# Two stacked expert layers behind a causal convolution: the sums of a block's end, the splits and the taps in another order

## The chip, the cores and the metric

The kernel runs on one core of one Trainium2 chip. The metric is the device time of one execution in microseconds (us), the median of several runs. TensorE (PE) multiplies, ScalarE (ACT) and VectorE (DVE) work on what it leaves in PSUM, GpSimd (POOL) helps at the start, and SyncE (SP) issues most transfers. Each engine takes its instructions in the order in which they stand in its queue.

## What is computed

The input `x` is 2 x 4096 x 192 in fp32. The cut reference:

```python
# layer "conv": softmax of 7 taps per head (8 heads of 24 channels), causal along the sequence
w = exp(weight - max(weight)); w = w / (sum(w) + 1e-09)
y[b, s, c] = sum_k w[head(c), k] * x_pad[b, s + k, c]
# first layer, 8192 tokens, 192 -> 2048 -> 192, weights in fp64
h = y @ w_in;  y1 = (h * sigmoid(h)) @ w_out
# second layer, the same shapes
h = y1 @ w_in2; out = where(h > 0, h, exp(min(h, 0)) - 1) @ w_out2
```

## The kernel before

Channels lie on partitions and tokens along the free dimension. 8192 tokens make 16 blocks of 512 (`b`); the 2048 hidden channels make 8 groups of 256 (`q`). A **unit** is (layer, block, q), 256 units in all: layer 0 is the SiLU layer, layer 1 the ELU layer. Each value is carried as a high and a low part. In layer 0 blocks 0 to 2 are computed with wide parts; from block 3 (`NEW`) on, in both layers, parts in fp16 with a scale per block are used for what goes into the second product, and in layer 0 also for `x` and both weights (the **narrow** weights, made by `rescale_in` and `rescale_out` from the wide ones during units 19 to 31).

**A unit.** `in_products` (line 595) makes `h`, two PSUM banks, of which there are two pairs; so the `h` of a unit can begin only when the `h` of two units ago has been read for the last time. `act_steps` then issues, in layer 0, Silu (ACT, line 643), the high part `g_hi` (ACT, 635) and the low part `lo` (DVE, 638), which reads `h` last. In layer 1 it issues Relu and Exp (ACT, 646 and 647), the joining `g` (DVE, 648), which reads `h` last, and then the high and low parts of the unit before, which were held back.

**Sums.** `high_products` (707) and `low_ab` (729) add a unit's part to four PSUM banks: `c0`, `c1` (64 of the 192 output channels and their low parts) and `ab0`, `ab1` (the other 128), the two of a name being the sums of two halves of the rows. Products trail `h` by three units (`LATE`). A **block's end** is the step whose trailing unit has q = 7: there `end_products` issues the block's low `c` products (719), the last high ones and the last `low_ab`, and the four banks have to be emptied before the next block opens them. `end_steps` returns `end_c` and `end_ab`: each copies one half with ACT (line 837, into `both`, `mid_ab` or `o`) and adds the other with DVE (line 828). `emit_end_c` then folds the two row halves of `both` into `other` (ACT 861, DVE 863). Layer 0 stores `mid_ab` and `other` to a buffer in DRAM, layer 1 stores `o` and `other` as the output.

**Work beside it.** `fill` is a table written by hand: `at(step, f, part)` files a piece of work under a unit's step and a part, and `run_fill(step, parts)` issues it. In an ordinary step all of a step's parts come ahead of the unit's activations; at a block's end part 0 comes ahead of them, part 1 between `end_c` and `end_ab`, and part 2 last. It holds the convolution's **taps** of later blocks (`conv_steps`, 14 per block, on DVE, lines 544 and 546), `found_it` (the reductions of `x`, 463), `set_scale` (line 486 and six more small DVE operations, giving `x_up`), `split_conv` (ACT 376, DVE 377: the two parts of a block's `x`, then exchanges of row halves by SP, 337), `split_mid` (the same for layer 1, from the stored block: two ACT copies, two DVE subtractions, a reduction, exchanges), and the decoding of layer 1's weights (`made_steps`; mag on ACT, lines 147, 151, 155 on DVE, a copy, subtractions) in layer 0's blocks 7 to 15. `split_mid` of layer 1's block b falls on a block's end, the one six units ahead of the block.

The scale of a block also goes out to DRAM and comes back as a broadcast (`share`, `fetch`) between its reduction and `set_scale`.

Of the kernel before, what the change touches and what calls it, by code (L numbers as in the profile page):

```python
# [37 lines left out]
NEW = 3  # L38
# [7 lines left out]
def kernel(  # L46
# [395 lines left out]
    def scaled(layer, b):  # L442
        return layer == 1 or b >= NEW
# [158 lines left out]
    def products(streams):  # L602
        for pair in zip(*streams):
            for f in pair:
                f()
# [270 lines left out]
    TWO = 2 * NQ  # L876
# [4 lines left out]
    def at(step, f, part=0):  # L881
        fill.setdefault((max(step, 0), part), []).append(f)
# [9 lines left out]
    def run(*lists):  # L892
        for fs in zip_longest(*lists):
            for f in fs:
                if f:
                    f()
# [14 lines left out]
    for b in range(2, NB):  # L911
        s = where[0, b, 0]
        if b > 2:
            at(s - 14, lambda b=b: pending.extend(x_loads(b)) if b < 5 else load_x(b))
        steps = [f for fs in zip(*(conv_steps(b, g) for g in range(2))) for f in fs]
        found_it = lambda b=b: measure(0, b, x_raw[b][:, 0, :], x_raw[b][:, 1, 0 : HT + PAD])
        splits = [lambda b=b, g=g: split_conv(b, g) for g in range(2)]
        if b < NEW:
            spread(steps + splits, s - 10, 8)
        elif b == 3:  # L920
            at(s - 10, found_it)
            spread(steps, s - 10, 6)
        elif b == 4:
            at(22, found_it)
            for k, f in enumerate(steps):
                at((22, 22, 22, 23, 23, 23, 24, 24, 24, 24, 25, 26, 27, 27)[k], f)
        else:
            at(s - 9, found_it)
            for k, f in enumerate(steps):
                step = s - 8 if k < 1 else s - 7 if k < 2 else s - 6  # L930
                at(step, f, 0 if k < 5 else 1 if k < 10 else 2)
        if b >= NEW:
            at(s - 7 + (b == NEW), lambda b=b: fetch((0, b)), int(b == NEW))
            at(s - 5 + (b == NEW), lambda b=b: set_scale(0, b))
            for f in splits:
                at(s - 4, f, int(b == NEW))
    for b in range(NB):
        at(where[1, b, 0] - 9, lambda b=b: load_mid(b))
        at(where[1, b, 0] - 6, lambda b=b: split_mid(b), 1)
# [5 lines left out]
    at(TWO + 1, lambda: fetch(0, nc.gpsimd))  # L945
    at(TWO + LAG, lambda: finish_weight_scale(0))
    for q in range(NQ):
        at((19, 20, 21, 22, 24, 25, 27, 29)[q], lambda q=q: rescale_in(q))
        at((21, 23, 24, 26, 28, 29, 30, 31)[q], lambda q=q: rescale_out(q))
    looks = [(b, *n) for b in range(3, 6) for n in ((7, 13), (8, 14), (9, 16))][:NQ]  # L950
    looks[:3] = (3, 9, 13), (3, 10, 14), (3, 11, 16)
    for q, (b, load, look) in enumerate(looks):
# [7 lines left out]
    for k, q in enumerate(range(NQ)):  # L960
        s = where[0, 8 + k, 0]
# [5 lines left out]
    with tc.manual_schedule():  # L967
# [174 lines left out]
        for s in range(4, TWO + 3):  # L1142
            both_products(s)
            if s == TWO + 2:
                pair_end(0)
                pair_end(1)
            act = act_steps(units[s])
            q = s // 2 + 1
            if s < 6:
                run(d_out[s - 2])  # L1150
                run(act[:-1])
                split_out(s - 2)
            elif q < NQ:
                if s % 2:
                    split_w(0, q, BOTH, nc.gpsimd)
                else:
                    run(decode_steps(0, q, BOTH, mag=mag_0))
            if s < 7:
                pending.extend(w_loads(0, s + 1))
            run_fill(s)  # L1160
            run(act[-1:] if s < 6 else act)

        for f in pending:
            f()
# [2 lines left out]
        act = act_steps(units[TWO + 3])  # L1167
        run_fill(TWO + 3)
        run(act)
        products(out_products(units[TWO + 1]))  # L1170

        turn = where[0, NEW, 0] + LAG
        for s in range(TWO + 4, n_units):
            u = units[s]
            if s < n_units - 2:
                products(in_products(u))
            if s in (n_units - 3, n_units - 2):
                if s == n_units - 3:
                    products(high_products(units[s - LATE]))
                products(in_products(units[s + 1]))  # L1180
            act = act_steps(u)
            done = units[s - (LATE if turn < s < n_units - 3 else LAG)]
            new = scaled(*done[:2])
            if s == turn or done[2] < NQ - 1:
                run_fill(s)
                run(act)
                if s != turn:
                    products(high_products(done) if new else out_products(done))
                    if new and done[:2] != (1, NB - 1):
                        low_ab(done, False)  # L1190
                continue
            if new:
                run_fill(s, 0)
                run(act)
                end_products(done)
            else:
                run(act[:1])
                products(out_products(done))
            both, end_c, end_ab = end_steps(*done[:2])
            end_c()  # L1200
            if not new:
                run(act[1:])
                run_fill(s, 0)
            run_fill(s, 1)
            end_ab()
            emit_end_c(*done[:2], both)
            run_fill(s, 2)

        products(high_products(units[-2]))
        for u in units[-NQ:-SOLE]:  # L1210
# [54 lines left out]
```

## Time and profile before

| | |
|---|---|
| median of 3 runs | 1123.03 us (1122.97 to 1123.32) |
| the profiled execution | 1122.6 us |
| its span in the profile | 1120.9 us |
| mean granted clock of PE | 0.992 |
| PE busy | 1066.7 us, 95% |
| DVE busy | 829.9 us, 74% |
| ACT busy | 813.4 us, 73% |

The profile is one execution. Its span goes from the first to the last instruction; the time of the execution is 1.7 us longer. Busy shares are means over stages of different kinds, and matmuls overlap one another, so their busy time does not say how densely they follow. A unit's length is read from the starts of the first `h` matmul of two units that follow each other. The granted clock is 1.00 at 2.4 GHz and 0.5 at 1.2 GHz.

### The profile page before, as it was taken

To read this page: it belongs to the slowest core of one execution; us is meant where nothing else is said; L and a number is where in the kernel's file an instruction comes from. 1 tells how busy PE (TensorE), PEld (TensorE's weight loads), DVE (VectorE), ACT (ScalarE), POOL (GpSimd) and SP (SyncE) were. 2 spreads that over 40 slices of the span, in tenths; PEclk is the share of its full clock that TensorE was granted. 3 is DMA by queue.
4 is the path that set the end of the run, shared out by engine and by line. 5 is a ranking of instruction groups with operands and counts; after the bars stand their busy time and mean duration, and the time that the engine had idled before them with its cause. 6 is when DMAs were issued, how large, how long until landed. Compare 5 with 4: busy or idle time off the path is not lost.

```text
span 1120.9 us, 23120 instructions
## 1 busy us (share of the span) xinstructions
PE 1066.7 (95%) x9763; PEld 681.5 (61%) x9763; DVE 829.9 (74%) x1166; ACT 813.4 (73%) x892; POOL 64.8 (6%) x95
## 2 busy tenths in 40 slices
PE   9999999999999999999999999999999999999998
PEld 6997544444444444444666667666776667766675
DVE  8998977777877778776477676776767677667776
ACT  7665766666667676667677787777877778777785
POOL 4420011101000000000000000000000000000000
PEclk9999999999999999999999999999999999999999
DMA  5412144423222322211222102221122211222101
GB/s 156 128 44 67 42 124 119 102 61 109 74 64 63 76 57 48 49 20 39 53 57 57 35 25 57 57 57 35 24 58 57 58 34 25 57 58 57 33 6 30
DMA packets 46520, 66.52 MB, mean 59 GB/s; under 512 B 10128, under 2 KB 25616, under 8 KB 46416
## 3 DMA queue, kind: packets, MB, share of 16 engines
q1 hardware_dynamic: 42416, 52.19, 19.3%
q0 software_dynamic: 4000, 12.85, 4.3%
q8 instruction: 76, 1.25, 0.5%
q14 instruction: 28, 0.23, 0.1%
HBM read 37.72 MB, written 12.61 MB: 45 GB/s over the span
## 4 chain that ended last, share of the span: by engine, by line
PE 65%; DVE 18%; ACT 10%; issue 5%; DMA 1%; SPq 0%; DVEq 0%; POOL 0%; ACTq 0%; POOLq 0%
PE h L595 37%; PE ab L707 13%; PE c L707 6%; PE ab L729 5%; DVE conv L546 5%; DVE lo L638 2%; ACT g_hi L635 2%; ACT h L643 2%; ACT x_hl L376 2%; DVE sum L463 2%; DVE g L648 1%; ACT g L647 1%; ACT g L646 1%; PE ab L782 1%; DVE both L828 1%
## 5 line engine op out<-in xcount | busy, mean ns | idle before, releaser
L595 PE MATMUL h<-x_hl,wi 64*128 64x512 f32 x2592 | 395.3, 414 | 2.2 <-DVE g_lo L630 1.8
L595 PEld LDWEIGHTS h<-x_hl,wi 64*128 64x128 f32 x2592 | 307.9, 189 | 33.9 <-DVE g_lo L630 2.7
L648 DVE SCALAR_TENSOR_TENSOR g<-g,h 128x1024 f32<-128x1024 f32 x128 | 156.1, 1220 | 166.6 <-ACT g L647 165.8
L595 PE MATMUL h<-x_hl,w 64*128 64x512 f16 x1872 | 222.9, 376 | 4.0 <-DVE lo L638 1.6
L646 ACT ACTIVATE g<-h 128x1024 f32<-128x1024 f32 x128 | 130.7, 1021 | 111.9 <-PE h L595 111.9
L638 DVE SCALAR_TENSOR_TENSOR lo<-h,forth,g_hi 128x1024 f16<-128x1024 f32 x104 | 133.5, 1284 | 102.1 <-ACT g_hi L635 101.6
L707 PE MATMUL ab<-g_hi,wo 64*128 64x512 f16 x1024 | 155.0, 377 | 28.2 <-DVE o L828 26.3
L643 ACT ACTIVATE h<-h,h_down 128x1024 f32<-128x1024 f32 x104 | 113.0, 1086 | 85.5 <-PE h L595 85.2
L595 PEld LDWEIGHTS <-w 64*128 64x128 f16 x1872 | 104.4, 94 | 107.9 <-issue 14.2
L638 DVE SCALAR_TENSOR_TENSOR lo<-g,forth,g_hi 128x1024 f16<-128x1024 f32 x128 | 163.5, 1278 | 0.0
L707 PEld LDWEIGHTS <-wo 64*128 64x128 f16 x1536 | 80.2, 94 | 113.3 <-issue 47.4
L635 ACT ACTIVATE g_hi<-g,forth 128x1024 f16<-128x1024 f32 x126 | 142.9, 1134 | 0.0
L647 ACT ACTIVATE g<-g 128x1024 f32<-128x1024 f32 x128 | 135.6, 1059 | 4.1
L707 PE MATMUL ab<-g_hi,w 64*128 64x512 f16 x832 | 115.5, 376 | 14.2 <-DVE mid_ab L828 14.2
L707 PEld LDWEIGHTS <-w 64*128 64x128 f16 x1248 | 68.8, 94 | 86.7 <-issue 25.5
L635 ACT ACTIVATE g_hi<-h,forth 128x1024 f16<-128x1024 f32 x104 | 115.9, 1114 | 3.4
L546 DVE SCALAR_TENSOR_TENSOR conv<-x_raw,tap_w,conv 128x512 f32<-128x512 f32 (+1 forms) x174 | 100.5, 632 | 0.2
L707 PE MATMUL c<-g_hi,wo 64*128 64x512 f16 x512 | 95.1, 381 | 0.0
L729 PE MATMUL ab<-lo,wo 64*128 64x512 f16 x484 | 94.1, 381 | 0.0
L729 PE MATMUL ab<-lo,w 64*128 64x512 f16 x416 | 68.5, 376 | 0.0
L707 PE MATMUL c<-g_hi,w 64*128 64x512 f16 x416 | 66.3, 377 | 0.0
L376 ACT ACTIVATE x_hl<-conv,x_up 64x256 f16<-64x256 f32 (+1 forms) x39 | 21.1, 573 | 42.1 <-DVE x_up L499 41.8
(146 smaller groups left out, 984.1 us busy)
## 6 DMA issues: line engine op xcount, KB each, us to landing
x_hl<-x_hl SPq DMA_DIRECT2D x34, 256.0 KB, 3.3
raw<-in_w_dram POOLq DMA_DIRECT2D x16, 512.0 KB, 4.8
x_raw<-in_xT_dram SPq DMA_DIRECT2D x16, 259.0 KB, 4.5
kept_ab<-mid_ab SPq DMA_DIRECT2D x16, 256.0 KB, 2.0
raw<-in_w_dram POOLq DMA_DIRECT2D x32, 128.0 KB, 3.4
mid_ab<-kept_ab SPq DMA_DIRECT2D x16, 256.0 KB, 4.9
mid_c<-kept_c SPq DMA_DIRECT2D x32, 128.0 KB, 4.9
x_hl<-x_hl SPq DMA_DIRECT2D x30, 128.0 KB, 2.4
```

The lines of the kernel that those rows point to most:

```text
L376: nc.scalar.activation(out=hi, in_=src, func=ACTF.Copy, scale=up_x)
L463: nc.vector.tensor_reduce(out=t if len(of) == 1 else t[:, k : k + 1], in_=x, axis=AX.X, op=ALU.max, apply_absolute_value=True)
L546: nc.vector.scalar_tensor_tensor(out=y, in0=x, scalar=w, in1=y, op0=ALU.mult, op1=ALU.add)
L595: nc.tensor.matmul(out=h[:, r, :], lhsT=w[ROWS[r], w_lo, ts(of, P)], rhs=x_part(layer, b, 3 * x_lo + part)[ROWS[r], :], start=n == 0, stop ...
L635: nc.scalar.activation(out=hi, in_=g, func=ACTF.Copy, scale=s)
L638: nc.vector.scalar_tensor_tensor(out=lo, in0=g, scalar=s, in1=hi, op0=ALU.mult, op1=ALU.subtract)
L643: silu = lambda: begun.append(nc.scalar.activation(out=g, in_=h, func=ACTF.Silu, scale=h_down[u[1]]))
L646: lambda: begun.append(nc.scalar.activation(out=g, in_=h, func=ACTF.Relu, scale=-1.0)),
L647: lambda: nc.scalar.activation(out=g, in_=g, func=ACTF.Exp, scale=-1.0),
L648: lambda: nc.vector.scalar_tensor_tensor(out=g, in0=g, scalar=-1.0, in1=h, op0=ALU.add, op1=ALU.max),
L707: nc.tensor.matmul(out=acc_t[layer, b, f"{name}{r}"], lhsT=wo[ROWS[r], i, ts(k, P)], rhs=hi[ROWS[r], i, :], start=q == 0 and n in (0, 2), ...
L729: nc.tensor.matmul(out=acc_t[layer, b, f"ab{r}"], lhsT=weights_of(u, 1)[ROWS[r], i, 0:P], rhs=g_t[u][1][ROWS[r], i, :], start=False, stop= ...
```

## The change

The taps of every block from 3 on are spread evenly, two to a unit: over seven units from ten units ahead of the block (six for blocks 3 and 4). `found_it` moves to the first of these units. The splits of `x` (blocks from 3 on) and the narrow weights get a part 3, which is issued behind a unit's activations. At a block's end of the scaled kind, `end_c` and `end_ab` follow one another, and parts 1 to 3 come behind; in layer 1 the last of the unit's activation steps, which is the held low part of the unit before, comes behind both too (`late`; in layer 0 the list is empty, since it is multiplied by the layer's number). No operation is added or taken away.

```diff
--- before.py
+++ after.py
@@ -920,20 +920,14 @@
         elif b == 3:
             at(s - 10, found_it)
             spread(steps, s - 10, 6)
-        elif b == 4:
-            at(22, found_it)
-            for k, f in enumerate(steps):
-                at((22, 22, 22, 23, 23, 23, 24, 24, 24, 24, 25, 26, 27, 27)[k], f)
         else:
-            at(s - 9, found_it)
-            for k, f in enumerate(steps):
-                step = s - 8 if k < 1 else s - 7 if k < 2 else s - 6
-                at(step, f, 0 if k < 5 else 1 if k < 10 else 2)
+            at(s - 10, found_it)
+            spread(steps, s - 10, 7 - (b == 4))
         if b >= NEW:
             at(s - 7 + (b == NEW), lambda b=b: fetch((0, b)), int(b == NEW))
             at(s - 5 + (b == NEW), lambda b=b: set_scale(0, b))
             for f in splits:
-                at(s - 4, f, int(b == NEW))
+                at(s - 4, f, 3)
     for b in range(NB):
         at(where[1, b, 0] - 9, lambda b=b: load_mid(b))
         at(where[1, b, 0] - 6, lambda b=b: split_mid(b), 1)
@@ -945,8 +939,8 @@
     at(TWO + 1, lambda: fetch(0, nc.gpsimd))
     at(TWO + LAG, lambda: finish_weight_scale(0))
     for q in range(NQ):
-        at((19, 20, 21, 22, 24, 25, 27, 29)[q], lambda q=q: rescale_in(q))
-        at((21, 23, 24, 26, 28, 29, 30, 31)[q], lambda q=q: rescale_out(q))
+        at((19, 20, 21, 22, 24, 25, 27, 29)[q], lambda q=q: rescale_in(q), 3)
+        at((21, 23, 24, 26, 28, 29, 30, 31)[q], lambda q=q: rescale_out(q), 3)
     looks = [(b, *n) for b in range(3, 6) for n in ((7, 13), (8, 14), (9, 16))][:NQ]
     looks[:3] = (3, 9, 13), (3, 10, 14), (3, 11, 16)
     for q, (b, load, look) in enumerate(looks):
@@ -1159,6 +1153,7 @@
                 pending.extend(w_loads(0, s + 1))
             run_fill(s)
             run(act[-1:] if s < 6 else act)
+            run_fill(s, 3)
 
         for f in pending:
             f()
@@ -1167,6 +1162,7 @@
         act = act_steps(units[TWO + 3])
         run_fill(TWO + 3)
         run(act)
+        run_fill(TWO + 3, 3)
         products(out_products(units[TWO + 1]))
 
         turn = where[0, NEW, 0] + LAG
@@ -1180,10 +1176,11 @@
                 products(in_products(units[s + 1]))
             act = act_steps(u)
             done = units[s - (LATE if turn < s < n_units - 3 else LAG)]
-            new = scaled(*done[:2])
+            new, late = scaled(*done[:2]), []
             if s == turn or done[2] < NQ - 1:
                 run_fill(s)
                 run(act)
+                run_fill(s, 3)
                 if s != turn:
                     products(high_products(done) if new else out_products(done))
                     if new and done[:2] != (1, NB - 1):
@@ -1191,7 +1188,8 @@
                 continue
             if new:
                 run_fill(s, 0)
-                run(act)
+                late = act[-1:] * done[0]
+                run(act[: len(act) - len(late)])
                 end_products(done)
             else:
                 run(act[:1])
@@ -1200,11 +1198,13 @@
             end_c()
             if not new:
                 run(act[1:])
-                run_fill(s, 0)
-            run_fill(s, 1)
+                run_fill(s, 0, 1)
             end_ab()
+            run(late)
+            if new:
+                run_fill(s, 1)
             emit_end_c(*done[:2], both)
-            run_fill(s, 2)
+            run_fill(s, 2, 3)
 
         products(high_products(units[-2]))
         for u in units[-NQ:-SOLE]:
```

How the order of instructions moves, at three places. First DVE at a block's end in layer 1 (`lo` is a low part, `both` and `o` are the two adds out of PSUM, the two lines 166 and line 463 are `split_mid`, `g` is the next unit's). Before:

```order
L648 SCALAR_TENSOR_TENSOR g<-g,h 128x1024
L638 SCALAR_TENSOR_TENSOR lo_9828<-g,forth,g_hi 128x1024
L828 SCALAR_TENSOR_TENSOR both<-c_9558,back,both 128x512
L166 TENSOR_TENSOR x_hl<-mid_ab,x_hl 128x512
L166 TENSOR_TENSOR x_hl<-mid_c,x_hl 128x512
L463 TENSOR_REDUCE sum<-x_hl 128x2
L828 SCALAR_TENSOR_TENSOR o<-ab_9560,back,o 128x512
L863 TENSOR_TENSOR other<-both,other 64x512
L648 SCALAR_TENSOR_TENSOR g<-g,h 128x1024
L638 SCALAR_TENSOR_TENSOR lo_9871<-g,forth,g_hi 128x1024
```

After:

```order
L648 SCALAR_TENSOR_TENSOR g<-g,h 128x1024
L828 SCALAR_TENSOR_TENSOR both<-c_9558,back,both 128x512
L828 SCALAR_TENSOR_TENSOR o<-ab_9560,back,o 128x512
L638 SCALAR_TENSOR_TENSOR lo_9828<-g,forth,g_hi 128x1024
L166 TENSOR_TENSOR x_hl<-mid_ab,x_hl 128x512
L166 TENSOR_TENSOR x_hl<-mid_c,x_hl 128x512
L463 TENSOR_REDUCE sum<-x_hl 128x2
L863 TENSOR_TENSOR other<-both,other 64x512
L648 SCALAR_TENSOR_TENSOR g<-g,h 128x1024
L638 SCALAR_TENSOR_TENSOR lo_9871<-g,forth,g_hi 128x1024
```

The add into `o` moves up from behind the reduction to directly behind that into `both`, and the low part of the unit before moves from ahead of both to behind them.

DVE at a block's end in layer 0, a block in the middle (`conv` are the taps). Before:

```order
L638 SCALAR_TENSOR_TENSOR lo_4358<-h,forth,g_hi 128x1024
L828 SCALAR_TENSOR_TENSOR both<-c_4040,back,both 128x512
L546 SCALAR_TENSOR_TENSOR conv<-x_raw,tap_w,conv 128x256
L546 SCALAR_TENSOR_TENSOR conv<-x_raw,tap_w,conv 128x512
L546 SCALAR_TENSOR_TENSOR conv<-x_raw,tap_w,conv 128x256
L546 SCALAR_TENSOR_TENSOR conv<-x_raw,tap_w,conv 128x512
L546 SCALAR_TENSOR_TENSOR conv<-x_raw,tap_w,conv 128x256
L828 SCALAR_TENSOR_TENSOR mid_ab<-ab_4042,back,mid_ab 128x512
L863 TENSOR_TENSOR other<-both,other 64x512
L546 SCALAR_TENSOR_TENSOR conv<-x_raw,tap_w,conv 128x512
L546 SCALAR_TENSOR_TENSOR conv<-x_raw,tap_w,conv 128x256
L546 SCALAR_TENSOR_TENSOR conv<-x_raw,tap_w,conv 128x512
```

After:

```order
L638 SCALAR_TENSOR_TENSOR lo_4318<-h,forth,g_hi 128x1024
L546 SCALAR_TENSOR_TENSOR conv<-x_raw,tap_w,conv 128x512
L546 SCALAR_TENSOR_TENSOR conv<-x_raw,tap_w,conv 128x256
L638 SCALAR_TENSOR_TENSOR lo_4364<-h,forth,g_hi 128x1024
L828 SCALAR_TENSOR_TENSOR both<-c_4038,back,both 128x512
L828 SCALAR_TENSOR_TENSOR mid_ab<-ab_4040,back,mid_ab 128x512
L863 TENSOR_TENSOR other<-both,other 64x512
L546 SCALAR_TENSOR_TENSOR conv<-x_raw,tap_w,conv 128x512
L546 SCALAR_TENSOR_TENSOR conv<-x_raw,tap_w,conv 128x256
L486 TENSOR_REDUCE total<-all 128x1
```

Between `both` and `mid_ab` no tap is left, a pair of taps stands ahead of each low part, and behind `other` come two taps, not four.

ACT in the two units behind such an end (line 643 is Silu, 635 the high part, 376 the split of `x`). Before:

```order
L861 ACTIVATE other<-both 64x512
L643 ACTIVATE h<-h,h_down 128x1024
L635 ACTIVATE g_hi<-h,forth 128x2x512
L376 ACTIVATE x_hl<-conv,x_up 128x512
L376 ACTIVATE x_hl<-conv,x_up 64x256 x2
L643 ACTIVATE h<-h,h_down 128x1024
L635 ACTIVATE g_hi<-h,forth 128x2x512
```

After:

```order
L861 ACTIVATE other<-both 64x512
L643 ACTIVATE h<-h,h_down 128x1024
L635 ACTIVATE g_hi<-h,forth 128x2x512
L643 ACTIVATE h<-h,h_down 128x1024
L635 ACTIVATE g_hi<-h,forth 128x2x512
L376 ACTIVATE x_hl<-conv,x_up 128x512
L376 ACTIVATE x_hl<-conv,x_up 64x256 x2
```

The split moves from ahead of a unit's two activations to behind them.

On SP the only move is that of the store of `mid_ab` or `o`, from behind the exchange of `x` halves and the share of the sum to ahead of them; PE's order is unchanged.

## Rows read from the trace of the kernel before

**Rows 1.** The page's head: span, then busy time, share and instructions of PE.

```profile
span 1120.9 us, 23120 instructions
...
PE 1066.7 (95%) x9763; PEld 681.5 (61%) x9763; DVE 829.9 (74%) x1166; ACT 813.4 (73%) x892; POOL 64.8 (6%) x95
```

**Rows 2.** PE's waits: engine, line, released by: us in total, times, longest.

```profile
PE ab L707 <- DVE o L828: 26.3, 14, 1.9
PE ab L707 <- DVE mid_ab L828: 16.1, 13, 1.9
```

**Rows 3.** Stretches from unit start to unit start: length, busy us by engine, granted clock, DMA.

```profile
155.48:489.95 334.47, 320.33 (x3043) 157.25 (x3040) 257.75 (x429) 224.00 (x242) 27.60 (x47) 1.00 0.30 78
592.31:1084.08 491.77, 465.46 (x4260) 331.43 (x4258) 345.16 (x392) 387.59 (x407) 0.00 (x0) 0.99 0.20 45
561.93:573.25 11.32, 9.44 (x71) 6.19 (x69) 7.84 (x10) 6.80 (x10) 0.00 (x0) 0.85 0.35 84
638.78:644.17 5.39, 5.39 (x39) 4.06 (x36) 1.96 (x2) 1.11 (x2) 0.00 (x0) 0.68 0.42 103
675.05:678.85 3.80, 3.80 (x38) 2.93 (x36) 1.95 (x2) 1.12 (x2) 0.00 (x0) 1.00 0.48 122
97.14:136.89 39.75, 36.37 (x318) 23.81 (x314) 38.12 (x75) 29.06 (x39) 0.00 (x0) 1.00 0.20 47
```

**Rows 4.** Timeline, layer 0, `h` of the five units behind a block's end: start, us.

```profile
361.80 2.11 PE L595 MATMUL h<-x_hl,w 64*128 64x512 f16 x18
...
366.85 2.30 PE L595 MATMUL h<-x_hl,w 64*128 64x512 f16 x18
...
371.00 2.12 PE L595 MATMUL h<-x_hl,w 64*128 64x512 f16 x18
...
374.93 2.12 PE L595 MATMUL h<-x_hl,w 64*128 64x512 f16 x18
...
378.60 0.61 PE L595 MATMUL h<-x_hl,w 64*128 64x512 f16 x4
```

**Rows 5.** Timeline around the same end: DVE, ACT and the waiting PE.

```profile
356.92 1.28 DVE L638 SCALAR_TENSOR_TENSOR lo<-h,forth,g_hi 128x1024 f16<-128x1024 f32 x1 [1.47 <-ACT g_hi L635]
...
362.00 0.69 ACT L837 ACTIVATE mid_ab<-ab,back 128x512 f32<-128x512 f32 x1 [0.61 <-PE ab L729]
...
362.44 2.59 DVE L546 SCALAR_TENSOR_TENSOR conv<-x_raw,tap_w,conv 128x256 f32<-128x256 f32 x5
...
364.95 0.74 DVE L828 SCALAR_TENSOR_TENSOR mid_ab<-ab,back,mid_ab 128x512 f32<-128x512 f32 x1
...
365.75 1.02 PE L707 MATMUL ab<-g_hi,w 64*128 64x512 f16 x7 [1.20 <-DVE mid_ab L828]
...
369.66 1.65 ACT L376 ACTIVATE x_hl<-conv,x_up 128x512 f16<-128x512 f32 x3 [3.47 <-DVE x_up L499]
```

**Rows 6.** Timeline around a block's end in layer 1.

```profile
809.44 2.43 PE L595 MATMUL h<-x_hl,wi 64*128 64x512 f32 x18
...
810.82 0.68 ACT L837 ACTIVATE o<-ab,back 128x512 f32<-128x512 f32 x1
...
812.49 1.22 DVE L463 TENSOR_REDUCE sum<-x_hl 128x2 f32<-128x1024 f32 x1
...
813.62 0.75 DVE L828 SCALAR_TENSOR_TENSOR o<-ab,back,o 128x512 f32<-128x512 f32 x1
...
814.41 1.02 PE L707 MATMUL ab<-g_hi,wo 64*128 64x512 f16 x7 [1.88 <-DVE o L828]
...
814.87 1.21 DVE L648 SCALAR_TENSOR_TENSOR g<-g,h 128x1024 f32<-128x1024 f32 x1
...
815.32 0.57 PE L595 MATMUL h<-x_hl,wi 64*128 64x512 f32 x1
```

**Rows 7.** Timeline, layer 0: the longer decode step and the two reductions on DVE.

```profile
344.89 0.96 DVE L155 SCALAR_TENSOR_TENSOR val<-mag,val 128x768 int32<-128x768 int32 x1
...
347.11 1.02 DVE L463 TENSOR_REDUCE sum<-x_raw 128x1 f32<-128x518 f32 x2
```

## The prediction

> **What bounds the kernel now.** I read the page's head first. TensorE (PE) is busy 1066.7 of 1120.9 us [rows 1], so PE sets the time, and a change is worth what it takes out of PE's stalls. The waits of PE name them: 26.3 us in 14 waits for the DVE add that ends `o`, 16.1 us in 13 waits for the one that ends `mid_ab` [rows 2]. Both are line 828, at a block's end: 13 ends in layer 0, 14 of 15 in layer 1. Idle rows alone miss part of the loss, since matmuls that start late or slowly count as busy, so I measured units by the start of the first `h` matmul.
>
> Layer 0, one block's end: `h` starts at 361.80, 366.85, 371.00, 374.93, 378.60 [rows 4]. The last distance, 3.67, is that of an undisturbed unit. The others are 5.05, 4.15 and 3.93, so an end loses 1.38 + 0.48 + 0.26 = 2.12 us. Ten blocks in a row take 334.47 us [rows 3], 33.45 each; eight units of 3.67 and 2.12 leave 1.97, the low `c` products of a block, which stay.
>
> Layer 1: an undisturbed unit is 3.80 us [rows 3], the one after an end 815.32 - 809.44 = 5.88 [rows 6]: 2.08 lost per end. Four times a unit of 5.39 follows, in which the granted clock is 0.68 against 1.00 [rows 3]: at 1.2 GHz for part of it instead of 2.4. Each directly follows a block end's stall, and so does a fifth, within 561.93 to 573.25 [rows 3].
>
> **Layer 1's ends.** Before, DVE's queue holds the low of the unit before, the split of the next block's `x` and its 1.22 us reduction between PE's last product and the add into `o`, which starts only at 813.62 [rows 6]. ACT's copy of the first `ab` half is behind two splits, at 810.82. PE idles 1.88 us and goes on at 814.41; it wanted the bank at 812.53. After, `o` stands directly behind `both`, and ACT's copy of `ab` loses the two split copies ahead of it. Even if that copy ended no earlier than it does now, at 811.50, the add behind it (0.75) would be done by 812.3, before PE asks; so the wait goes whole: 14 x 2.08 = **29.1 us**.
>
> What is late next? The low, split, reduction and `other` now stand ahead of the next unit's `g`, which before ran 814.87 to 816.08 [rows 6]. The work is the same; only a gap ahead of the two adds is new, where DVE used to run the low while ACT copied; I bound it by one add, 0.75, so `g` ends by 816.83. The bank it empties is wanted two units after 809.44, at 809.44 + 7.60 = 817.04. Covered by 0.2 us; without that cover an end costs what exceeds it. The unit after has only `g` and a low on DVE, so the delay dies out. The low is read two units later and the stored sum by nobody on the chip. On SP's queue the store of `o` moves ahead of the exchange of `x` halves and the reduction's share; the exchanged halves are wanted five units later, so I cost that at 0.
>
> **Half-clock stretches.** Four of 5.39 - 3.80 = 1.59 us: **6.4 us**. They stand only behind stalls of about 1.9 us (5 of 15 such) and never behind layer 0's 1.20. I take them as gone with the stalls; the other end of this term is 0.
>
> **The change of layers.** The two units from 561.93 take 11.32 us [rows 3] against 7.60: a stall of 1.88 (the longest `mid_ab` wait [rows 2]) and half clock. Same cure: **3.7 us**, of which some 1.6 hang on the clock.
>
> **Layer 0's ends.** Before, five taps (2.59 us from 362.44) stand between `both` and `mid_ab`, whose add starts at 364.95; PE idles 1.20 and goes on at 365.75 [rows 5]. Four more taps and the scale steps follow, so ACT waits 3.47 us for `x_up` ahead of its split of `x`, and that split stands in front of the next Silu [rows 5]: the 0.48 and 0.26. After, ACT's copy of `ab` still ends at 362.00 + 0.69 = 362.69, and DVE's add follows at once: done by 363.5, a microsecond before PE asks (364.55). Then come `other`, two taps and the scale steps instead of four taps. The split moves behind the next unit's low and finds `x_up` ready. All three losses go: eleven ends (the ten blocks and the one after) x 2.12 = **23.3 us**. The end with no taps but the first `split_mid` keeps what is left of 16.1 - 11 x 1.20 - 1.9 = **1.0 us**, which goes too.
>
> The taps are now two to a unit in seven units. A pair is about 1.04 (five take 2.59). Ahead of a low DVE used to sit idle 1.47 us in a quiet unit [rows 5], so a pair is covered. One unit per block is fuller: reductions (1.02), two first taps (at most a pair), two decode steps of layer 2's weights (0.96 the longer [rows 7]): at most 1.02 + 1.04 + 2 x 0.96 = 3.98. Room there: 3.67 - 1.28 = 2.39, and a low that ends 358.20 [rows 5] is wanted at 361.80 less 1.97, 1.63 later: 4.02 in all. This is the tightest place, in the seven blocks (7 to 13) that decode while taps run. The unit before it starts its low late too, because the moved split and the decode's magnitude stand before its Silu on ACT, so some of the room is already spent. I take 0.1 lost, with bounds 0 and 0.6: **-0.7 us** (0 to -4.2).
>
> **The start of narrow weights.** From 97.14 to 136.89 DVE is busy 38.12 of 39.75 us [rows 3]: there DVE is the bound. Moving narrow weights behind activations lets lows free `h` banks earlier, but the work stays. I take **+1.0 us** (a little of the 1.63 idle, and one narrow step of about 0.6 pushed past the last tight bank), bounds -1 and +3.
>
> **Sum.** 29.1 + 6.4 + 3.7 + 23.3 + 1.0 - 0.7 + 1.0 = 63.8 us. The profiled execution took 1122.6; 1122.6 - 63.8 = 1058.8. The median of the runs, 1123.03, is 0.4 above it: 1059.2, given as **1059 us**.
>
> The sum is larger than PE's idle time, 1120.9 - 1066.7 = 54.2 us [rows 1], because half-clock and staggered matmuls count as busy. The Trainium skill (Perfetto Trace Analysis, "Identifying the Most-Contended Engine") says matmul busy share is no good measure of the distance to the roofline, since pipelined matmuls look different in a trace; read as a ceiling, the busy share would cap the gain at 54.2 and the time at 1069. The spacing of units in this trace is on the page's side.
>
> **Rivals.**
> *The half clock stays.* For: most stalls of the same length are not followed by one, so the stall alone is not the cause. Against: none occurs without one. 1059 + 6.4 + 1.6 = 1067. The Trainium skill (TensorE: Matmul & The Clock Gate, "A second HAM failure mode: psum-queue depth-cycling") describes a matmul kernel that swings between both levels on brief idles between its groups; by that, what small gaps are left at an end could keep some stretches.
> *Lows stay late in layer 0.* The pair and the full unit use the room up, so 0.48 + 0.26 return at eleven ends (8.1) and the full unit costs 0.6 (another 3.5): 1071. For: 3.98 against 4.02. Against: 1.47 idle ahead of the low elsewhere.
> *Only the named waits go*, and a bank or the next activation takes the rest: 42.4 [rows 2], 1081. For: `g` has 0.2 us of cover in layer 1. Against: its delay does not add up over units.
> *Slower.* Taps in front of every low push each `h` bank. If a pair were exposed in full in six units of twelve blocks: 6 x 12 x 1.04 = 75, 1134; it would pass 1123 from 0.9 us exposed per unit. Against: the idle 1.47 is more than the pair.
> *It does not do what it says.* The order shows each move on DVE and ACT, so only a wait through a shared tile could undo it: 1123.
>
> **How the numbers follow.** Forecast 0.66, half clock 0.10, lows late 0.10, only the waits 0.08, slower 0.04, nothing 0.02. The range reaches from 1054, all front stalls gone, to 1071, which takes in the first two rivals and leaves out about 0.17 with a little of the forecast. Faster by over 0.2% (what a measurement of this kernel can tell from no change): 0.94; within: 0.02; slower: 0.04.
>
> **What would show it.** Waits of PE for line 828 gone in both layers; units after an end at 3.67 and 3.80; no unit of 5.39 and a granted clock of 1.00 throughout; `x_hl` no longer waiting for `x_up`. Wrong if PE's `h` matmuls start waiting for DVE's `lo` in blocks 7 to 13, or for `g` behind layer 1's ends, or if half-clock stretches show without a stall.

## The result, and the profile after

The changed kernel takes 1056.41 us (median of 4 runs, 1055.88 to 1056.56) against 1123.0 for the kernel before on the same chip (4 runs, 1121.81 to 1123.32): a ratio of 0.9408, with a 95% interval of 0.9392 to 0.9424. The forecast was 1059 us with a range of 1054 to 1071; it holds, with a gain that is 2.6 us larger. The profiled execution took 1055.88 us, so against the 1122.6 of the profile before there are 66.7 us to place.

The page's head of the profile after (span; busy time, share and instructions; granted clock in 40 slices), which answers to [rows 1]:

```profile
span 1054.2 us, 23130 instructions
...
PE 1044.8 (99%) x9763; PEld 601.7 (57%) x9763; DVE 831.3 (79%) x1166; ACT 814.2 (77%) x892; POOL 65.3 (6%) x95
...
PEclk9999999999999999999999999999999999999999
```

All of PE's waits in the profile after, which answer to [rows 2]:

```profile
PE h L595 <- DVE lo L638: 3.7, 3, 1.6
PE warm L966 <- POOL ones L963: 1.1, 1, 1.1
PE h L595 <- DMA x_hl<-x_hl: 0.2, 1, 0.2
```

Line 828 is gone from the list. What is left are three waits for a low part, 3.7 us in all, in units 27, 28 and 63. Stretches of the profile after, which answer to [rows 3] (length; busy us and instructions of PE, PEld, DVE, ACT, POOL; granted clock; DMA share, GB/s): the ten blocks of layer 0, the 14 blocks of layer 1, the two units at the change of layers, and one long unit in layer 0:

```profile
153.95:468.32 314.37, 313.30 (x3043) 141.12 (x3041) 257.65 (x429) 223.26 (x242) 27.58 (x47) 1.00 0.35 83
563.48:1017.61 454.13, 454.13 (x4261) 279.69 (x4258) 346.44 (x392) 388.65 (x407) 0.00 (x0) 1.00 0.21 49
531.06:538.66 7.60, 7.60 (x86) 4.76 (x84) 5.42 (x6) 6.92 (x9) 0.00 (x0) 1.00 0.01 2
268.20:273.11 4.91, 3.84 (x37) 1.65 (x34) 4.70 (x13) 1.93 (x4) 1.70 (x3) 1.00 0.15 16
```

In layer 1 PE is busy for the whole of its 454.13 us, with the clock at 1.00 (2.4 GHz) throughout. With the starts of the first `h` matmul of the same unit in both traces (units counted from 0), the whole gain is placed:

| from | to | before | after | gain | the sum's term |
|---|---|---|---|---|---|
| start | unit 34 (start of the narrow weights) | 155.48 | 153.95 | 1.5 | 1.0 |
| unit 34 | unit 122 (eleven ends of layer 0) | 367.92 | 345.68 | 22.2 | 23.3 - 0.7 |
| unit 122 | unit 130 (layer 0's last end) | 32.61 | 31.43 | 1.2 | 1.0 |
| unit 130 | unit 138 (change of layers) | 36.30 | 32.42 | 3.9 | 3.7 |
| unit 138 | unit 250 (14 ends of layer 1) | 491.77 | 454.13 | 37.6 | 29.1 + 6.4 |
| unit 250 | end | 36.82 | 36.55 | 0.3 | 0 |
| sum | | 1120.9 | 1054.2 | 66.7 | 63.8 |

A block's end in layer 1 in the timeline after (start, us, engine, line, operation, out<-in; in brackets the idle time before it and its releaser), which answers to [rows 6]:

```profile
758.00 2.42 PE L595 MATMUL h<-x_hl,wi 64*128 64x512 f32 x18
...
760.35 1.92 PE L719 MATMUL c<-lo,wo 64*64 64x512 f16 x32
...
763.75 2.43 PE L595 MATMUL h<-x_hl,wi 64*128 64x512 f32 x18
764.13 0.69 ACT L837 ACTIVATE o<-ab,back 128x512 f32<-128x512 f32 x1
...
764.88 0.74 DVE L828 SCALAR_TENSOR_TENSOR o<-ab,back,o 128x512 f32<-128x512 f32 x1
...
766.46 1.03 PE L707 MATMUL ab<-g_hi,wo 64*128 64x512 f16 x8
...
769.67 1.21 DVE L648 SCALAR_TENSOR_TENSOR g<-g,h 128x1024 f32<-128x1024 f32 x1
...
771.39 0.80 PE L595 MATMUL h<-x_hl,wi 64*128 64x512 f32 x4
```

The add into `o` ends at 765.62, 0.84 us before PE opens the bank again at 766.46, with no wait. The two units behind the end take 767.57 - 763.75 = 3.82 each. The next unit's `g` ends at 770.88, 0.51 ahead of the `h` at 771.39 that needs its bank.

The same in layer 0, which answers to [rows 5]:

```profile
380.21 0.69 ACT L837 ACTIVATE mid_ab<-ab,back 128x512 f32<-128x512 f32 x1 [0.61 <-PE ab L729]
...
380.93 0.75 DVE L828 SCALAR_TENSOR_TENSOR mid_ab<-ab,back,mid_ab 128x512 f32<-128x512 f32 x1 [0.18 <-ACT mid_ab L837]
...
382.39 1.03 PE L707 MATMUL ab<-g_hi,w 64*128 64x512 f16 x8
...
384.39 0.15 DVE L499 TENSOR_TENSOR x_up<-forth,fro 128x1 f32<-128x1 f32 x1
...
384.59 1.28 DVE L638 SCALAR_TENSOR_TENSOR lo<-h,forth,g_hi 128x1024 f16<-128x1024 f32 x1
385.79 1.14 DVE L546 SCALAR_TENSOR_TENSOR conv<-x_raw,tap_w,conv 128x512 f32<-128x512 f32 x2
...
387.96 1.64 ACT L376 ACTIVATE x_hl<-conv,x_up 128x512 f16<-128x512 f32 x3
```

`mid_ab` is out of PSUM at 381.68, 0.71 before PE asks at 382.39, and the split of `x` starts at 387.96 without a wait, 3.4 us behind `x_up`. The `h` of these units starts at 380.01, 383.68, 387.35, 391.02: 3.67 apart, where [rows 4] had 5.05, 4.15 and 3.93.

### The profile page after: what moved, and what is told of

The parts are those of the page before. It is cut to its first block, busy times and chain, and to the rows that moved or that the text cites. A ratio compares the mean times of both kernels' runs of the same rounds, so it can differ in the third digit from the quotient of the medians.

```text
span 1054.2 us, 23130 instructions
## 1 busy us (share of the span) xinstructions
PE 1044.8 (99%) x9763; PEld 601.7 (57%) x9763; DVE 831.3 (79%) x1166; ACT 814.2 (77%) x892; POOL 65.3 (6%) x95
## 4 chain that ended last, share of the span: by engine, by line
PE 90%; DVE 5%; ACT 2%; issue 1%; DMA 1%; SPq 0%; POOL 0%; ACTq 0%; DVEq 0%; POOLq 0%
PE h L595 45%; PE ab L707 19%; PE c L707 10%; PE ab L729 9%; PE c L719 5%; PE ab L782 1%; PE c L782 1%; DVE conv L546 1%; DVE found L216 1%; DVE g_lo L630 1%; DVE lo L638 1%; DMA all<-shared 0%; DVE more L243 0%; ACT x_hl L376 0%; PE last L746 0%
## 5 line engine op out<-in xcount | busy, mean ns | idle before, releaser
L595 PE MATMUL h<-x_hl,wi 64*128 64x512 f32 x2592 | 366.8, 407 | 0.2 <-DMA x_hl<-x_hl 0.2
L595 PEld LDWEIGHTS h<-x_hl,wi 64*128 64x128 f32 x2592 | 260.9, 185 | 62.6 <-DMA x_hl<-x_hl 0.6
L595 PEld LDWEIGHTS <-w 64*128 64x128 f16 x1872 | 93.0, 94 | 113.2 <-issue 5.3
L707 PE MATMUL ab<-g_hi,wo 64*128 64x512 f16 x1024 | 131.4, 376 | 0.0
L707 PEld LDWEIGHTS <-wo 64*128 64x128 f16 x1536 | 64.9, 94 | 96.4 <-issue 35.4
L707 PE MATMUL ab<-g_hi,w 64*128 64x512 f16 x832 | 106.9, 376 | 0.0
L707 PEld LDWEIGHTS <-w 64*128 64x128 f16 x1248 | 60.3, 94 | 75.5 <-issue 5.9
L707 PE MATMUL c<-g_hi,wo 64*128 64x512 f16 x512 | 77.5, 381 | 0.0
L729 PE MATMUL ab<-lo,wo 64*128 64x512 f16 x484 | 72.0, 376 | 0.0
L729 PE MATMUL ab<-lo,w 64*128 64x512 f16 x416 | 62.0, 376 | 0.0
L628 ACT ACTIVATE g_hi<-h 128x1024 fp32r<-128x1024 f32 x22 | 22.6, 1027 | 26.1 <-PE h L595 24.4
```

Of the source, the lines that this page charges most:

```text
L595: nc.tensor.matmul(out=h[:, r, :], lhsT=w[ROWS[r], w_lo, ts(of, P)], rhs=x_part(layer, b, 3 * x_lo + part)[ROWS[r], :], start=n == 0, stop ...
L628: lambda: nc.scalar.activation(out=hi, in_=h, func=ACTF.Silu),
L707: nc.tensor.matmul(out=acc_t[layer, b, f"{name}{r}"], lhsT=wo[ROWS[r], i, ts(k, P)], rhs=hi[ROWS[r], i, :], start=q == 0 and n in (0, 2), ...
L729: nc.tensor.matmul(out=acc_t[layer, b, f"ab{r}"], lhsT=weights_of(u, 1)[ROWS[r], i, 0:P], rhs=g_t[u][1][ROWS[r], i, :], start=False, stop= ...
```

## Experiments

Each kernel is given by what it changes of the changed kernel, unless it says otherwise. Times are medians, and each ratio is to the kernel before on the same chip.

**Each half of the change alone.** First the new ends with the old table of taps, splits and narrow weights:

```diff
         else:
-            at(s - 10, found_it)
-            spread(steps, s - 10, 7 - (b == 4))
+            at(s - 9, found_it)
+            for k, f in enumerate(steps):
+                step = s - 8 if k < 1 else s - 7 if k < 2 else s - 6
+                at(step, f, 0 if k < 5 else 1 if k < 10 else 2)
...
             for f in splits:
-                at(s - 4, f, 3)
+                at(s - 4, f, int(b == NEW))
```

> The changed kernel with the old table of fill: the order at a block's end is the new one, while taps, the splits of x and the narrow weights stand where they stood before. My account: layer 1 needs the ends alone, so its gain stays whole. In layer 0 the five taps only slide from between the two adds to behind them; ahead of the next low part DVE still has nine taps and the scale steps, so h of the second unit behind an end starts when it did before (some 371.0 on the old trace) and the 2.12 us per end are lost again, as a wait for lo instead of for mid_ab: 1056.4 + 11 x 2.12 + about 1.5 at the start of the narrow weights = 1081 us. Rival (each named wait is worth its own length): the 1.20 of each end in layer 0 is gained and only 0.92 lost: 1056.4 + 11 x 0.92 + 1.5 = 1068 us.

Measured: 1086.47 us, ratio 0.9686 (0.9672 to 0.9701). The account had the place right, the rival fell, and the cost in layer 0 is larger than both. In layer 1 every stall is gone, and its units are as long as in the changed kernel. In layer 0 an end costs more than before. PE waits for a low 13 times, 23.3 us in all. DVE and PE behind one end, in the timeline:

```profile
368.23 2.59 DVE L546 SCALAR_TENSOR_TENSOR conv<-x_raw,tap_w,conv 128x256 f32<-128x256 f32 x5
...
371.35 2.19 DVE L546 SCALAR_TENSOR_TENSOR conv<-x_raw,tap_w,conv 128x512 f32<-128x512 f32 x4
...
374.79 1.28 DVE L638 SCALAR_TENSOR_TENSOR lo<-h,forth,g_hi 128x1024 f16<-128x1024 f32 x1
...
376.13 1.24 PE L595 MATMUL h<-x_hl,w 64*128 64x512 f16 x9 [1.98 <-DVE lo L638]
```

The sum leaves PSUM in time, but the nine taps are still in the queue ahead of the next low, and PE waits for that low's bank: 2.14 + 0.26 = 2.40 per end, where it was 2.12. Three of these eleven stalls are followed by a half-clock stretch, which layer 0 had not had. Then the other half, the new table with the old order at an end:

```diff
-                late = act[-1:] * done[0]
-                run(act[: len(act) - len(late)])
+                run(act)
...
+            run_fill(s, 1)
             end_ab()
-            run(late)
-            if new:
-                run_fill(s, 1)
             emit_end_c(*done[:2], both)
```

> The changed kernel with the old order at a block's end; taps, splits and narrow weights stand as in the changed kernel. In layer 0 both orders are the same, since no fill is left between the adds. My account: layer 0's 23 us stay gained, layer 1's go: 1056.4 + 14 x 2.08 + 14 x 0.2 (the end unit is 0.2 shorter in the changed kernel) + half-clock stretches behind some of the stalls (4 to 5 of 1.6) + 2.1 at the change of layers + 1.0 = 1098 to 1100 us. Rival (the taps alone do nothing, the adds' order is what counts in both layers): about 1123.

Measured: 1097.38 us, ratio 0.9781 (0.9765 to 0.9798). PE's wait for the sum of layer 1 in it:

```profile
PE ab L707 <- DVE o L828: 26.2, 14, 1.9
```

Layer 0 is at 3.67 a unit, and layer 1 keeps its stalls and four half-clock stretches. Alone the halves gain 35.1 and 24.2 us; the whole gained 66.6 on its own chip, some 7 more than both. That is about layer 0's loss in the first run, whose eleven ends take 375.29 us against 367.92 in the kernel before: 11 x 0.28 for the longer stalls and 3 x 1.42 for the half clock, 7.3. In layer 0 the table does the work (345.67 us with the old ends, 345.68 with the new), and the new end without it only moves the wait.

**The late low.**

```diff
-                late = act[-1:] * done[0]
+                late = []
```

> The changed kernel without its late low part: in layer 1 the low part of the unit before stands ahead of the two adds again; the adds follow one another all the same. My account: the add into o ends by 812.3 on the clock of the old trace, 0.2 before PE asks, so nothing changes: 1056.4 within 0.5 us. Rival (the low part in front keeps DVE from c for so long that PE waits again): up to 0.7 per end in 14 ends, 1066 us.

Measured: 1055.66 us, ratio 0.941 (0.9396 to 0.9424), with no new wait. Holding the low back behind both sums is worth nothing that the runs can tell.

**Only `split_mid` back between both sums.**

```diff
+            if new:
+                run_fill(s, 1)
             end_ab()
             run(late)
-            if new:
-                run_fill(s, 1)
```

> The changed kernel with layer 1's split between the two adds again, the low part still behind both. Without the low part ahead the stall is shorter than before: some 0.7 to 1.2 us instead of 1.88 at 14 ends, 1.9 and 1.0 at the last two of layer 0. My account (half clock follows only stalls near 1.9 us): no half-clock stretch in layer 1, 1056.4 + 14 x (0.7 to 1.2) + 14 x 0.2 + 3 = 1072 to 1079 us. Rival (half clock follows any stall, one in three): the same plus 4 or 5 stretches of 1.6: 1079 to 1087 us.

Measured: 1082.81 us, ratio 0.9653 (0.9638 to 0.9667). PE waits 1.16 at each of 14 ends, and none of them is followed by half clock. Beside that it keeps the 3.7 us at the change of layers and 1.2 us at layer 0's last end. At an end of layer 1 in its timeline:

```profile
577.95 0.38 PE L707 MATMUL ab<-g_hi,wo 64*128 64x512 f16 x1
...
579.49 1.02 PE L707 MATMUL ab<-g_hi,wo 64*128 64x512 f16 x7 [1.16 <-DVE o L828]
...
580.15 0.59 PE L729 MATMUL ab<-lo,wo 64*128 64x512 f16 x3
...
580.40 0.58 PE L595 MATMUL h<-x_hl,wi 64*128 64x512 f32 x1
...
580.56 0.38 PE L729 MATMUL ab<-lo,wo 64*128 64x512 f16 x1
580.59 1.77 PE L595 MATMUL h<-x_hl,wi 64*128 64x512 f32 x12
```

These rows show a cost that the prediction's sum did not have. One `ab` matmul of eight runs at 577.95, and the other seven only after the wait. From there on the groups are interleaved: the first `h` matmul starts ahead of the last `L729`. The kernel issues its matmuls of 64 rows in pairs, one of each row half. In the trace after, both of a pair start within 0.003 us (758.000 and 758.003), and the next pair some 0.23 later. Behind a stall the halves are one step apart: in the trace before, the `h` matmuls from 804.34 on start one by one, 0.07 and 0.16 apart in turn. That lasts through the block and ends at the low `c` products (719, 64*64 tiles): the end unit here takes 5.93 us, against 5.75 in the changed kernel. The kernel before shows the same at an end in layer 1:

```profile
803.53 0.57 PE L595 MATMUL h<-x_hl,wi 64*128 64x512 f32 x1
...
806.04 1.92 PE L719 MATMUL c<-lo,wo 64*64 64x512 f16 x32
```

Line 719 starts 2.51 behind the unit's `h`. [rows 6] has the same torn `h` group at 815.32. In the changed kernel, where that group is one row of 18 at 758.00, the low `c` products start 760.35 - 758.00 = 2.35 behind it. So each stall of layer 1 costs another 0.19 at the next block's end. All layer 1 end units are 5.91 to 5.97 in the kernel before, the second and the fourth run, where the ends stall, and 5.75 in the changed kernel and the first run, where they don't. The cause itself, which half waits and why the low `c` products bring them together, was read from the rows and not tried.

**A longer stall.** The split between both sums, and two more reductions of the same 1.2 us behind it:

```diff
+            if new:
+                run_fill(s, 1)
+            if new and done[0] == 1 and (1, done[1] + 2) in x_hl:
+                spare = small(2, tag="spare")
+                for _ in range(2):
+                    nc.vector.tensor_reduce(
...
             end_ab()
             run(late)
-            if new:
-                run_fill(s, 1)
```

> The kernel of the run before (layer 1's split between the two adds) with two more reductions into a spare tile ahead of the add into o, 1.13 us each in DVE's queue: the stall at 14 ends grows from 1.16 to about 3.4 us. The two reductions are additional work and their result is not used. If the chance of half clock grows with the length of a stall (0 of 14 at 1.16, about a third at 1.9), most of the ends are now followed by a stretch: 8 to 14 of 14, 1082.8 + 14 x 2.26 + (8 to 14) x 1.6 = 1127 to 1137 us. Rival (a stall only has to be longer than some length, then one in three): 4 or 5 of 14, 1121 to 1122 us.

Measured: 1138.11 us in one run, against 1122.21 for the kernel before. PE waits 49.6 us in 14 waits, 3.5 each. Two pairs of units behind an end in its stretches:

```profile
648.29:660.91 12.62, 9.08 (x71) 5.57 (x69) 10.27 (x12) 6.78 (x10) 0.00 (x0) 0.86 0.42 88
685.92:700.07 14.15, 10.60 (x71) 6.83 (x69) 10.28 (x12) 6.78 (x10) 0.00 (x0) 0.76 0.49 107
```

In 14 of 14 such pairs the clock is 0.87 or lower. The pairs take 182.6 us together, 56.8 more than 14 pairs of the run before (5.16 + 3.83); 14 x (3.5 - 1.16) = 32.8 of it is stall, and 24.0, 1.7 per end, is the clock's.

**The splits of `x` ahead of the activations again.**

```diff
             for f in splits:
-                at(s - 4, f, 3)
+                at(s - 4, f, int(b == NEW))
```

> The changed kernel with the splits of x ahead of a unit's activations again. My account: with two taps instead of four behind an end, x_up is ready as early as the copy can start, so blocks from 5 on lose nothing (Silu 0.4 later, covered); the split of block 3, issued while DVE is the bound, stops ACT for some 5 us as before: 2 us in all, 1058.4 us, within 1057.4 and 1059.4. Rival (the 0.26 us that an end lost to the split in front of Silu return in eleven blocks): 1056.4 + 2.9 + 2 = 1061 us.

Measured: 1069.03 us, ratio 0.9531 (0.9517 to 0.9546). Both theories missed: they looked at `x_up`, which is early enough, and not at the taps. ACT's wait, then the timeline behind one end:

```profile
ACT x_hl L376 <- DVE conv L546: 23.9, 11, 2.2
```

```profile
363.46 1.14 DVE L546 SCALAR_TENSOR_TENSOR conv<-x_raw,tap_w,conv 128x512 f32<-128x512 f32 x2
...
364.23 1.65 ACT L376 ACTIVATE x_hl<-conv,x_up 128x512 f16<-128x512 f32 x3 [2.17 <-DVE conv L546]
...
365.91 1.09 ACT L643 ACTIVATE h<-h,h_down 128x1024 f32<-128x1024 f32 x1
...
368.18 1.28 DVE L638 SCALAR_TENSOR_TENSOR lo<-h,forth,g_hi 128x1024 f16<-128x1024 f32 x1 [1.53 <-ACT g_hi L635]
...
369.51 1.69 PE L595 MATMUL h<-x_hl,w 64*128 64x512 f16 x14 [0.66 <-DVE lo L638]
```

With two taps to a unit, the last pair stands in the unit of the split, behind a low on DVE. A split ahead of the activations waits 2.17 for that pair, and Silu, the low and PE wait behind it: 0.82 us in each of eleven units, 9.0. The even taps need the later split. Against the changed kernel on that chip (1055.63, below) the run loses 13.4 us; the other 4 lie ahead of unit 34, whose `h` starts at 158.01, where ACT waits up to 5.3 us for `x_up`. Some 1.75 of these 4 are half clock: behind a wait of PE of 1.83 us, unit 22 takes 6.06 us, where it takes 4.31 in the changed kernel. Its stretch:

```profile
108.21:114.27 6.06, 6.06 (x38) 4.79 (x40) 5.79 (x11) 4.74 (x7) 0.00 (x0) 0.72 0.06 14
```

**The narrow weights ahead of the activations again.**

```diff
-        at((19, 20, 21, 22, 24, 25, 27, 29)[q], lambda q=q: rescale_in(q), 3)
-        at((21, 23, 24, 26, 28, 29, 30, 31)[q], lambda q=q: rescale_out(q), 3)
+        at((19, 20, 21, 22, 24, 25, 27, 29)[q], lambda q=q: rescale_in(q))
+        at((21, 23, 24, 26, 28, 29, 30, 31)[q], lambda q=q: rescale_out(q))
```

> The changed kernel with the narrow weights ahead of a unit's activations again. My account: DVE is the bound from unit 20 to unit 29 and its work is the same, so the end of this stretch moves by less than one narrow step in the queue: 0.3 to 1.5 us more, 1056.7 to 1057.9 us. Rival (all that the start has gained, 1.5 us by the start of unit 34's h, and the 0.6 us at unit 20 hang on this part): 1058.5 us.

Measured: 1056.88 us (1056.76 to 1059.11), ratio 0.943 (0.9414 to 0.9445). By the medians that is 0.5 us over the changed kernel's first four runs and 1.3 over those on this chip (1055.63, below), and the intervals of the ratios overlap. The `h` of unit 34 starts at 155.12, against 153.95 and 154.32 in two profiles of the changed kernel. But it starts anywhere from 153.77 to 155.03 in six other runs that leave this stretch as the changed kernel has it: the second to the fifth, the eighth, and the ninth. So how much of the front's gain is this move's stays unclear. PE's longest wait for a low is here 2.71 us, and the stretch behind it stays at full clock:

```profile
132.67 2.12 PE L595 MATMUL h<-x_hl,w 64*128 64x512 f16 x18 [2.71 <-DVE lo L638]
```

```profile
132.67:136.78 4.11, 3.84 (x35) 1.91 (x34) 3.97 (x12) 1.92 (x2) 0.00 (x0) 1.00 0.13 28
```

**How full the fullest unit is.** Two reductions of 128 x 512, whose results nothing uses, are added to the unit that takes a block's own reductions, in six blocks of layer 0:

```diff
+    def spare_work(b):
+        spare = small(2, tag="spare")
+        for k in range(2):
+            nc.vector.tensor_reduce(
...
+    for b in range(10, NB):
+        at(where[0, b, 0] - 10, lambda b=b: spare_work(b))
```

> The changed kernel with two more reductions (0.53 us each in the queue, into a spare tile, their result not used) in the fullest unit of blocks 8 to 13 in layer 0. In the changed kernel one such unit, in block 7, also holds the scale of the second layer's weights, 1.45 us, and the h two units on is 1.24 late; so the room is 0.2 us, and each of six units now costs 1.06 - 0.2 = 0.85: 1056.4 + 5.1 = 1061.5 us. Rival (the room is the 0.6 that I kept as the bound): 6 x 0.45 = 2.7, 1059 us. Rival (no queue of DVE is near its limit there): 1056.4 us.

Measured: 1062.94 us, ratio 0.9478 (0.9464 to 0.9492). DVE's queue in one of these units (line 958 is the added work), then PE behind it:

```profile
366.90 0.74 DVE L544 TENSOR_SCALAR conv<-x_raw,tap_w 128x512 f32<-128x512 f32 x2
367.56 1.27 DVE L958 TENSOR_REDUCE spare<-x_raw 128x1 f32<-128x512 f32 x2
...
371.59 1.69 PE L595 MATMUL h<-x_hl,w 64*128 64x512 f16 x14 [0.98 <-DVE lo L638]
```

Of 1.27 us added, 1.14 come back as a longer unit (4.81 against 3.67), six times. So 0.13 us of room is left there.

**A piece of work out of the fullest unit, and a better table.** In the profile after, the long unit at 268.20 is such a unit, into which the scale of layer 2's second output weight falls once: 1.29 us from 268.98, of which 1.24 show in the unit's 4.91. These rows of the profile after show it:

```profile
268.98 0.41 DVE L515 TENSOR_REDUCE most<-all 128x2 f32<-128x256 f32 x1
...
271.77 1.28 DVE L638 SCALAR_TENSOR_TENSOR lo<-h,forth,g_hi 128x1024 f16<-128x1024 f32 x1
...
273.11 2.12 PE L595 MATMUL h<-x_hl,w 64*128 64x512 f16 x18 [1.07 <-DVE lo L638]
```

Three kernels on one chip: the scale one unit earlier, the same with two more edits of the table, and the changed kernel once more.

```diff
-    at(look + 8, lambda: finish_weight_scale(1))
+    at(look + 7, lambda: finish_weight_scale(1))
```

> The changed kernel with one edit: the scale of layer 2's second output weight (a reduction and six small DVE operations, 1.29 us, 268.98 to 270.27 in the trace after) is filed one unit earlier, out of block 7's fullest unit into the one ahead of it. Theory (the fullest units have no room at all, the unit ahead has some): the 4.91 us of unit 63 become 3.67, 1.24 less: 1055.2 against 1056.4. Rival (the unit ahead of it is as full, since both reductions and a pair of taps stand near there): the loss only moves, 1056.4, and the long unit stands one earlier.

```diff
-            spread(steps, s - 10, 7 - (b == 4))
+            spread(steps, s - 10, 7)
...
-        at((21, 23, 24, 26, 28, 29, 30, 31)[q], lambda q=q: rescale_out(q), 3)
+        at((22, 23, 25, 28, 29, 30, 31, 32)[q], lambda q=q: rescale_out(q), 3)
...
-    at(look + 8, lambda: finish_weight_scale(1))
+    at(look + 7, lambda: finish_weight_scale(1))
```

> The changed kernel with three edits to the table: the scale of layer 2's second output weight one unit earlier as in the run beside it; block 4's taps over seven units from ten units ahead of it instead of six; the eight narrow parts of the first output weight in units 22, 23, 25, 28, 29, 30, 31, 32 instead of 21, 23, 24, 26, 28, 29, 30, 31. Theory (units 23, 27 and 28 are long because a pair of taps and a narrow weight's subtraction meet on DVE ahead of a low, 4.58, 5.43 and 4.91 instead of 3.67): the two waits of 1.58 and 1.06 there shrink by some 2.5 in all, with 1.24 from the scale, 1052.7. Rival (DVE is the bound through all of this stretch, so the work only moves to other units): 1055.2, the scale's part alone.

> The changed kernel once more, for the same chip as the two beside it. All theories: 1056.4, 1055.9 to 1056.9.

Measured: 1054.45 us (1054.27 to 1055.53), 1054.8 (1054.01 to 1055.52) and 1055.63 (1055.35 to 1056.21), ratios 0.9402, 0.9403 and 0.9411. The scale's unit falls from 4.92 to 3.74, and the median by 1.18, as expected, though the highest run of the one, 1055.53, lies above the lowest of the other, 1055.35. The other two edits give nothing that can be told. PE waits 2.6 us in two waits for a low with the scale alone, and 2.4 us in one with all three edits. The two long units, 5.42 and 4.91 (10.33 together), become 6.34 and 3.67 (10.01). Nearly all of that work only moves, so the rival held there. The kernel with the scale one unit earlier has the lowest median of all, 1.2 us below the changed kernel, and the shorter unit accounts for it; from the kernel with all three edits it cannot be told.

## Why the prediction was right, point by point

- **PE is the bound, and the stalls at a block's end are the price.** Right. With line 828 out of PE's waits, the two layers run at 3.67 and 3.82 a unit.
- **Layer 1's ends, 29.1.** The step held, `o` being out 0.84 us before PE asks. The term was too small: units behind an end went from 5.88 to 3.82, 28.8 us, but the end units also went from about 5.94 to 5.75, 14 x 0.19 = 2.7 us. The sum left the end unit as long as it was in the trace, and it carried the stagger of the stall one block earlier. That one step is most of the 2.9 us by which the sum was short.
- **`g` as the next in line, covered by 0.2.** Right in kind; the cover is 0.51.
- **Half clock, 6.4.** Right: four units of 5.39 became 3.82, 6.3 us, and no stretch is left. The rival that it stays fell. The Trainium skill (TensorE: Matmul & The Clock Gate, "A second HAM failure mode: psum-queue depth-cycling") speaks of swings on brief idles; here 14 waits of 1.16 us kept none, so no run here shows it for gaps that short.
- **Change of layers, 3.7.** Measured 3.9, with the same 0.17 of stagger.
- **Layer 0's ends, 23.3.** Right in size: 22.2 and the 1.24 of the next point are 23.5. One reason was incomplete. I gave `x_up` as what the split waits for; with the new taps it is the last pair, and only the place behind the activations hides that (9 us in the sixth run).
- **The fullest unit, 0.7.** The estimate of the room (4.02 against 3.98) was near, 0.13 measured, and six of the seven blocks lost nothing, where I took 0.1 each. What I left out is the seventh, in which the scale of a layer 2 weight falls into that unit: 1.24 us. Both are inside the bounds. In that place one sign of being wrong did show, an `h` that waits for a low in blocks 7 to 13: once, 1.07 us at 273.11. And of the signs of being right one held only in part: `x_hl` still waits for `x_up` once, 1.6 us at the start of layer 0.
- **Narrow weights, 1.0.** Measured 1.5 for the stretch up to unit 34; that the size came out is in part luck. The sum had only the narrow weights in it, and putting them back costs 0.5 to 1.3 us by the medians. Block 3's split and block 4's taps move in the same stretch, and the sum gave them nothing; putting the splits back costs some 4 us there (sixth run). How the 1.5 divides among these moves is not shown.
- **Ceiling by busy share, 1069.** It fell: 66.7 us were gained, with 54.2 of idle PE. PE's idle time fell by 44.8 us and its busy time by 21.9 (1066.7 to 1044.8): half-clock and staggered matmuls were counted as busy, as the sum said.
- **The other rivals.** Only the named waits (1081) fell, since all that stood behind them went too. Lows late in layer 0 (1071) is seen in the first run and in the sixth; in the changed kernel only in the one unit named above. Slower (1134) fell too: with a pair of taps ahead of the lows the units of layer 0 are 3.67.
- **One loss that no step had.** In the profile after, one unit of layer 1 (at 941.10) takes 4.13, because the scale of a block comes back from DRAM late and DVE waits for it:

```profile
942.61 0.42 DVE L486 TENSOR_REDUCE total<-all 128x1 f32<-128x256 f32 x1 [2.10 <-DMA all<-shared]
```

  The same kernel once more shows 3.81 there, so it comes and goes with the transfer.

## What to carry to other kernels

Where one engine is the bound and works ahead into a few PSUM banks, let whatever empties a bank stand first in the other engines' queues, and then look for what the work that was moved back meets there: here the new ends alone cost layer 0 7.4 us more, evenly spread taps gave all of its 22.2 with either order of the ends, and 9 of these needed the split behind the activations. Price a stall by the length of all units until the pattern repeats, not by the wait: a wait of 1.88 us cost 2.08 at once, 0.19 a block later and now and then 1.6 of half clock. Busy share of the bounding engine was no ceiling for the gain.

## What the runs showed of the hardware

- **Behind the long stalls of the blocks' ends half clock was frequent, behind the short ones it did not occur.** In the traces of the kernel before and of the first, second, fourth and fifth run, stalls of 1.16 to 1.20 us were followed by a stretch in which part of the granted clock was at 1.2 GHz in 0 of 25 cases, stalls of about 1.9 us in 10 of 32, the 2.0 us stalls of layer 0 in the first run in 3 of 11, and 3.5 us (one run) in 14 of 14. A stretch cost 1.4 to 1.7 us. Length alone does not decide: at the start of layer 0, a stall of 1.83 us in the sixth run was followed by one, and one of 2.71 us in the seventh was not. Why stalls of like length differ stays open.
- **In layer 1 a one-sided wait staggered the two row halves of TensorE for the rest of a block.** The unit in which they come together again was 0.19 us longer, about the same behind stalls of 1.16 us (5.93) and of 1.88 (5.94). In layer 0 the cost does not show: in the kernel before, a pair's matmuls start 0.02 us apart up to the block's end, and the end units are 5.64 with the stalls against 5.62 to 5.64 without.
